# Decoding an output weight by columns and moving its decode phases into later steps (sparse attention followed by a token mix)

## The chip, the cores and the metric

The kernel runs on one core of one Trainium2 chip. The metric is the time of one launch in microseconds (us), measured on the device. Three runs of the kernel before gave 586.12 us in the median (585.53 to 589.59).

## The reference

Two parts follow each other. The first is block-sparse attention over 4 batches, 8 heads, 768 tokens and a head width of 64. The second is a mix over tokens on the result `x` (4 x 768 x 512):

```python
theta = x @ w_theta                       # 512 x 512
zr, zi = x * cos(theta), x * sin(theta)
y = einsum('ts,bsd->btd', w_tok_r, zr) + einsum('ts,bsd->btd', w_tok_i, zi)
u = x + y
return u + maximum(u @ w_ch, 0)           # w_ch is 512 x 512
```

The weights are float64 (q, k and v float32). The host only rearranges them, so the kernel itself turns the 64-bit words of each weight into pairs of fp32r tiles (a high part and a low part). A product with such a weight takes three matmuls: high by high, high by low, low by high.

## The kernel before, in words

**Decoding.** A `Piece` (line 50) is a run of columns of one weight: it loads the words (`load`, line 61, a DMA on SP's queue into a `raw` tile, two buffers), and is then decoded in three phases. Phase 0 is one ACT instruction (`start`, line 68) and three DVE instructions (`bits`, lines 72 to 74). Phase 1 is two DVE instructions (`rest`, lines 80 and 82). Phase 2 is one ACT copy that writes the high part (`high`, line 88) and two DVE instructions (`low`, lines 91 and 92), the second of which writes the low part. `Decoder.go(n)` (line 116) issues the next n phases; after the last phase of a piece it issues the load of the piece after next, since that one takes over its `raw` buffer. `Decoder.ahead(n)` (line 107) issues the ACT instructions that can go before.

**Which pieces.** Most weights are decoded during attention. Twelve pieces of 256 columns, 36 phases, are left for the token mix: four pieces hold the last 512 columns of `w_tok_r` and `w_tok_i` (columns 256 to 767 of the sixth token block, which only the product steps with j = 5 read), eight hold `w_ch`. Its tile is `[128, 4, 512]`: four blocks c of input channels by 512 output columns. Before, a piece of `w_ch` is 256 consecutive elements of that tile read as one row, that is half of one block c.

**Steps.** `token_mix` (line 586) runs 48 steps: k = 12 b + 6 h + j for batch b, half h of the channels and token block j. In step k, `theta(k + 2)` (12 matmuls of 256 columns), `reduced`, `waves`, `turned` (ACT and DVE work on the angles: range reduction, cosine and sine, product with x, split into high and low) prepare steps ahead; `turn` and `split` (DVE transposes, line 638, ACT cast, line 646, DVE difference, line 647) prepare x of step k + 3 where h is 0; `mix(k)` issues 24 matmuls of 384 columns that add into four accumulators `y` (lines 707 to 709). After j = 5, `add_x` (lines 720 to 723) makes `u`.

**Output products.** `out(b, th, e)` (line 725) makes 128 output columns e for 384 tokens th: 12 matmuls (lines 730 to 732) that read the column block e of all four blocks c of `w_ch`, then two DVE instructions (735 and 736) and a store on SP's queue. The eight products of a batch are put on `pending` at its last step and issued two by two in steps j = 1 to 4 of the next batch, in one PSUM buffer. The order is all four e for th = 0, then all four for th = 1.

**What sets the order.** Attention and the first five steps (`FIXED`, line 787) stand under a manual schedule: each engine gets them in the order of the program text. From step 5 on, a planner that simulates the engines orders the instructions of each engine, with the program text as priority; it also fills gaps of the manual part with work from later steps. Each engine's queue is then fixed and in order. `PHASES` (line 30) says how many phases each of the steps 0 to 12 gets: 2, 3, 3, 4, 4, 0, 4, 4, 4, 3, 3, 0, 2. The first 12 phases are the four `w_tok` pieces, so before they end with step 3.

In a fixed step the decode phases stand behind the step's other work and ahead of its products:

```python
turned(k + 1); split(k + 3); reduced(k + 2); load(k + 3); load_raw(k + 5)
decoder.ahead(PHASES[k]); decoder.go(PHASES[k])
mix(k)
```

Of the kernel before, what the change touches and what calls it, by code (L numbers as in the profile page):

```python
# [10 lines left out]
F32 = mybir.dt.float32  # L11
# [5 lines left out]
ALU = mybir.AluOpType  # L17
# [9 lines left out]
Q_BUFS = 3  # L27
XO_BUFS = 2
FIXED = 5
PHASES = (2, 3, 3, 4, 4, 0, 4, 4, 4, 3, 3, 0, 2)  # L30
LATER = 2560


# [16 lines left out]
class Piece:  # L50
# [4 lines left out]

    def __init__(self, nc, place, part, src, name):
        self.nc, self.place, self.part, self.src, self.name = nc, place, part, src, name
        self.f = src.shape[1] // 2
        self.before = None

    def load(self, pool, queue):
        self.raw = pool.tile([P, self.f, 2], I32, tag="raw", name=f"raw_{self.name}", bufs=2)
        queue.dma_start(self.raw, self.src.rearrange("p (f w) -> p f w", w=2))

    def start(self, pool):
        self.pool = pool
# [17 lines left out]
    def high(self):  # L84
        if self.before:
            self.before()
        self.hi, self.lo = [x.rearrange("p c f -> p (c f)")[:, self.part] for x in self.place]
        self.nc.scalar.copy(self.hi, self.a)

    def low(self):  # L90
        self.nc.vector.tensor_tensor(self.a, self.a, self.hi.bitcast(F32), op=ALU.subtract)
        self.nc.vector.tensor_tensor(self.lo, self.a, self.raw[:, :, 0].bitcast(F32), op=ALU.add)


class Decoder:
# [490 lines left out]
def token_mix(tc, w, ch_pieces, xs, outT, bias, nb, fore):  # L586
# [7 lines left out]
    nc = tc.nc  # L594
    with ExitStack() as late, ExitStack() as ctx:
# [4 lines left out]
        def at(k):  # L600
            return k // 12, (k // 6) % 2, k % 6

        def load(k):

            b, h, j = at(k)
            xa[k] = xp.tile([P, 4, 4, 32], F32, tag="xa", name=f"xa{k}")
            for i in range(4):
                src = xs[b // 2][4 * j + i, :, :, b % 2].rearrange("c q p f -> q c (p f)")
                dst = xa[k][32 * i : 32 * i + 32].rearrange("s (c p) x u -> s c (p x u)", c=2)
                nc.sync.dma_start(dst, src)  # L610

        def load_raw(k, pool=None, parts=range(4)):

            b, h, j = at(k)
            if h:
                return
            if pool is not None:
                xr[b, j] = pool[:, 512 * j : 512 * j + 512].rearrange("p (i c u) -> p i c u", i=4, c=4)
            else:
                xr[b, j] = zp.tile([P, 4, 4, 32], F32, tag="xr", name=f"xr{b}_{j}", bufs=2)  # L620
            for p in parts:
                src = xs[b // 2][4 * j : 4 * j + 4, p // 2, :, b % 2, p % 2].rearrange("i q c -> q i c")
                nc.sync.dma_start(xr[b, j][32 * p : 32 * p + 32].rearrange("r i c u -> r i (c u)"), src)
# [69 lines left out]
        def turned(k):  # L693
            multiplied(k)
            highs(k)
            lows(k)
# [28 lines left out]
        def out(b, th, e, pool, tag):  # L725
            ps = pool.tile([P, 384], F32, tag=tag, name=f"o{b}_{th}_{e}")
            wh, wl = [x[:, :, 128 * e : 128 * e + 128] for x in w["ch"]]
            for c in range(4):
                uh, ul = [t[:, c % 2, :] for t in us[b, c // 2, th]]
                nc.tensor.matmul(ps, wh[:, c, :], uh, start=c == 0, stop=False)  # L730
                nc.tensor.matmul(ps, wh[:, c, :], ul, start=False, stop=False)  # L731
                nc.tensor.matmul(ps, wl[:, c, :], uh, start=False, stop=c == 3)  # L732
            uh, ul = [t[:, e % 2, :].bitcast(F32) for t in us[b, e // 2, th]]
            o = wk.tile([P, 384], F32, tag="o", name=f"of{b}_{th}_{e}")
            nc.vector.tensor_tensor(o, uh, ul, op=ALU.add)
            nc.vector.scalar_tensor_tensor(o, ps, 0.0, o, op0=ALU.max, op1=ALU.add)
            nc.sync.dma_start(outT[b, 128 * e : 128 * e + 128, 384 * th : 384 * th + 384], o)

        vp = yield
        place = vp.tile([P, 6, 260], F32, tag="vw", name="xr_first").rearrange("p c f -> p (c f)")  # L740
# [5 lines left out]
        decoder = Decoder(ch_pieces(), None, nc.sync, fore)  # L746
# [5 lines left out]
        for k in range(2):  # L752
            load(k)
# [19 lines left out]
        split(2)  # L773
        highs(0)
        load(2)
        yield
        lows(0)
# [8 lines left out]
        pending = []  # L786
        for k in range(FIXED):
# [7 lines left out]
            load_raw(k + 5)  # L795
            phases = PHASES[k]
            decoder.ahead(phases)
# [6 lines left out]
        for k in range(FIXED, steps):  # L804
            b, h, j = at(k)
            if k + 4 < steps:
                load(k + 4)
            if k + 5 < steps:
                load_raw(k + 5)
            if k + 2 < steps:  # L810
                theta(k + 2)
                reduced(k + 2)
                waves(k + 2)
                turned(k + 2)
            if k + 3 < steps:
                turn(k + 3)
                split(k + 3)
            if k < len(PHASES):
                decoder.ahead(PHASES[k])
                decoder.go(PHASES[k])  # L820
            mix(k)
            if h == 0 and b > 0 and 0 < j < 5:
                for _ in range(2):
                    out(*pending.pop(0), ps_o, "o")
            if h == 1 and j == 5:
                pending += [(b, th, e) for th in range(2) for e in range(4)]
        while pending:
            out(*pending.pop(0), ps_y, "y")

# [1 line left out]
def sparse_attention_then_token_mix(ctx, tc, qT, qE, kT, vr, sampled, w_theta, w_tok_r, w_tok_i, w_ch, outT):  # L831
    nc = tc.nc
    n_batch = outT.shape[0]
    const = ctx.enter_context(tc.tile_pool(name="const", bufs=1))
    ident = const.tile([P, P], F32, name="ident")
    make_identity(nc, ident)
    bias = []
    for name, value in (("half_pi", math.pi / 2), ("up_int", ROUND), ("down_int", -ROUND), ("early", 0.0)):
        bias.append(const.tile([P, 1], F32, name=name))
        nc.vector.memset(bias[-1], value)  # L840
    dram = ctx.enter_context(tc.tile_pool(name="dram", bufs=1, space=bass.MemoryType.DRAM))
    xs = [dram.tile([NB, 2, 32, 2, 2, P], F32, name=f"xs{bp}") for bp in range(NP)]

    w = {}
    w["theta"] = [const.tile([P, 4, 512], F32R, name=f"w_theta_{x}") for x in ("hi", "lo")]
    for name in ("tok_r", "tok_i"):
        w[name] = [const.tile([P, 2, 768], F32R, name=f"w_{name}_{x}") for x in ("hi", "lo")]

    def room(name, use, dtype=F32):
        return const.tile([P, 8, 768], dtype, tag=f"room_{name}", name=f"{use}_{name}")  # L850

    def settle(name):
        t = room(name, "w", F32R)
        w[name] = [x[:, j] for x in w[name] for j in range(2)]
        w[name] = [w[name][2 * x : 2 * x + 2] + [t[:, 4 * x + j] for j in range(4)] for x in range(2)]
        return [t[:, 4 * x : 4 * x + 4] for x in range(2)]

    words = {n: a.bitcast(I32) for n, a in dict(theta=w_theta, tok_r=w_tok_r, tok_i=w_tok_i, ch=w_ch).items()}

    def pieces(name, f, place, at=0, span=None):  # L860
        made = []
        first, last = span or (0, place[0].shape[1] * place[0].shape[2])
        for f0 in range(first, last, f):
            f1 = min(f0 + f, last)
            made.append(Piece(nc, place, slice(f0, f1), words[name][:, 2 * (at + f0) : 2 * (at + f1)], f"{name}_{at + f0}"))
        return made


    fore = ctx.enter_context(tc.tile_pool(name="fore", bufs=2))
    rests = dict(tok_r=[], tok_i=[])  # L870

    def mix_pieces():
        made = [x for n, place in rests.items() for x in pieces(n, 256, place, 1536, (LATER, 3072))]
        return made + pieces("ch", 256, w["ch"], span=(0, 2048))

    follow = token_mix(tc, w, mix_pieces, xs, outT, bias, n_batch, fore)
    next(follow)
    early = pieces("theta", 512, w["theta"])
    early += [x for pair in zip(pieces("tok_r", 512, w["tok_r"]), pieces("tok_i", 512, w["tok_i"])) for x in pair]
    for name, place in rests.items():  # L880
        made = pieces(name, 512, place, 1536, (0, LATER))
        made[0].before = lambda name=name, place=place: place.extend(settle(name))
        early += made
    attention(tc, qT, qE, kT, vr, sampled.bitcast(I32), xs, ident, early, room, follow)
    for _ in follow:
        pass
# [48 lines left out]
```

## Time and profile before

| | |
|---|---|
| three timed runs, median | 586.12 us (585.53 to 589.59) |
| profiled execution: its own time | 591.45 us |
| profiled execution: span from first to last instruction | 589.7 us |
| busy share of the span: PE, DVE, ACT, POOL | 92%, 75%, 58%, 26% |
| mean granted TensorE clock | 0.988 |
| decode instructions of `w_ch` (`da_ch` tiles) | first at 281.0 us, last at 339.7 us |
| output product matmuls (lines 730 to 732) | first at 290.0 us, last at 585.3 us |
| loads of `w_ch` words | 8 of 256 KB, issued from 276.8 to 322.3 us |

Times in the profile are us from the start of the span. PE is TensorE's matmuls and PEld its weight loads, which overlap matmuls; DVE is VectorE, ACT ScalarE, SPq the queue of SyncE that issues DMAs. A row of the timeline gives start, duration, engine, source line, operation, what it writes from what it reads, shape, and in brackets the idle time of the engine before it with what ended it. A row of a table by stretches gives for each engine its busy time and, in brackets, how many instructions, then the granted clock (PEclk), the share of DMA time and GB/s. Matmul ends are modelled.

### The profile page before, as it was taken

The numbers are of one execution on the slowest core, as the hardware profiler recorded it, in microseconds if no ns is written. First come the engines' busy times: TensorE is split into PE (matmuls) and PEld (weight loads), VectorE is DVE, ScalarE is ACT, GpSimd is POOL, SyncE is SP. The second block draws the span as 40 slices with busy tenths as digits, with TensorE's granted clock in tenths as the row PEclk, the third lists the DMA queues.
The fourth block names the chain that finished last, engine by engine and source line by source line (L and its number), as shares of the span: only waits on it lengthen the run. The fifth ranks groups of instructions, "written<-read, shape, count | busy, mean of one in ns | idle before, by whom it ended". The sixth has DMA issues, their size and how long they took to land.

```text
span 589.7 us, 16811 instructions
## 1 busy us (share of the span) xinstructions
PE 541.2 (92%) x6636; PEld 477.0 (81%) x6636; DVE 440.0 (75%) x1011; ACT 344.1 (58%) x734; POOL 150.7 (26%) x262
## 2 busy tenths in 40 slices
PE   4898887998988978989999999999999999999997
PEld 1565654666666656878998999999999999999997
DVE  2687985887889878889989996648857549547554
ACT  2686775858797868755766544456534547434510
POOL 1467885741689874000000000000000000000000
PEclk9998998999999989999999999999999999999999
DMA  8979999886799997544323242111432111212002
GB/s 288 345 207 329 287 353 359 266 256 243 218 303 302 301 303 208 138 133 126 107 72 107 83 143 82 58 50 55 131 94 68 50 53 43 79 56 73 4 1 107
DMA packets 63551, 95.60 MB, mean 162 GB/s; under 512 B 9200, under 2 KB 44656, under 8 KB 63472
## 3 DMA queue, kind: packets, MB, share of 16 engines
q1 hardware_dynamic: 57136, 71.09, 39.1%
q0 software_dynamic: 6336, 23.43, 12.1%
q8 instruction: 52, 0.85, 0.6%
q14 instruction: 27, 0.22, 0.1%
HBM read 81.90 MB, written 12.58 MB: 160 GB/s over the span
## 4 chain that ended last, share of the span: by engine, by line
PE 59%; DVE 15%; issue 6%; POOL 6%; ACT 5%; DMA 3%; POOLq 2%; SPq 2%; DVEq 0%; ACTq 0%
PE y L709 8%; PE y L707 8%; PE y L708 8%; POOL kg L270 5%; PE o L731 4%; PE o L732 4%; PE o L730 4%; PE T L326 4%; PE X L360 3%; PE S L309 3%; PE h L657 3%; PE h L655 3%; PE h L656 3%; PE SW L402 2%; DVE m L311 2%
## 5 line engine op out<-in xcount | busy, mean ns | idle before, releaser
L320 ACT ACTIVATE P<-S,m 128x256 f32<-128x256 f32 x176 | 69.2, 486 | 6.6 <-DVE m L311 6.3
L328 ACT COPY pT<-T 128x1024 f32<-128x1024 f32 x44 | 44.7, 1017 | 33.2 <-PE T L326 32.6
L311 DVE TENSOR_REDUCE m<-S 128x4 f32<-128x1024 f32 x44 | 53.5, 1217 | 13.3 <-PE S L309 13.2
L326 PE MATMUL T<-ident,P 128*128 128x128 f32 x352 | 52.5, 291 | 9.3 <-ACT P L320 3.2
L270 POOL COPY kg<-kb 128x256 f32 (+2 forms) x101 | 53.3, 569 | 16.2 <-PE S L309 16.1
L270 POOL COPY kg<-kb_tok_i 128x256 f32 (+2 forms) x101 | 50.8, 543 | 25.2 <-DVE sb_scratch L176 15.2
L326 PEld LDWEIGHTS T<-ident,P 128*128 128x128 f32 x352 | 40.3, 147 | 21.0 <-ACT pT L328 10.9
L662 ACT ACTIVATE t<-h,up_int 128x256 f32<-128x256 f32 x48 | 22.6, 473 | 57.2 <-PE h L657 55.9
L655 PE MATMUL h<-w_theta_hi,xTh 128*128 128x256 f32 x192 | 54.3, 283 | 1.7 <-ACT xTh L646 1.7
L657 PE MATMUL h<-w_theta_hi,xTl 128*128 128x256 f32 x192 | 54.1, 282 | 0.4 <-DVE xTl L647 0.4
L309 PE MATMUL S<-kg,q 64*32 64x256 f32 x1408 | 51.0, 393 | 3.7 <-issue 2.2
L292 POOL DMA_INDIRECT vb<-in_vr_dram,rows x44 | 44.5, 1012 | 37.3 <-PE X L360 31.2
L656 PE MATMUL h<-w_theta_lo,xTh 128*128 128x256 f32 x192 | 53.9, 281 | 0.0
L707 PE MATMUL y<-w_tok_r,zh 128*128 128x384 f32 x128 | 43.3, 338 | 2.2 <-ACT zh L687 2.2
L731 PE MATMUL o<-ul,w_ch_hi 128*128 128x384 f32 x128 | 43.0, 336 | 0.4 <-DVE ul L723 0.4
L708 PE MATMUL y<-w_tok_i,zh 128*128 128x384 f32 x128 | 43.1, 337 | 0.0
L709 PE MATMUL y<-w_tok_r,zl 128*128 128x384 f32 x128 | 43.1, 337 | 0.0
L707 PE MATMUL y<-w_tok_i,zh 128*128 128x384 f32 x128 | 43.1, 336 | 0.0
L708 PE MATMUL y<-w_tok_r,zh 128*128 128x384 f32 x128 | 43.0, 336 | 0.0
L732 PE MATMUL o<-uh,w_ch_lo 128*128 128x384 f32 x128 | 42.9, 335 | 0.0
L672 ACT ACTIVATE cs<-rr 128x256 f32<-128x256 f32 x48 | 20.0, 416 | 39.3 <-DVE rr L667 39.3
L730 PE MATMUL o<-uh,w_ch_hi 128*128 128x384 f32 x128 | 42.5, 336 | 0.0
(155 smaller groups left out, 1432.1 us busy)
## 6 DMA issues: line engine op xcount, KB each, us to landing
xa<-xs SPq DMA_DIRECT2D x192, 64.0 KB
out_dram<-of SPq DMA_DIRECT2D x32, 192.0 KB
va<-in_vr_dram SPq DMA_DIRECT2D x22, 260.0 KB
q<-in_qT_dram SPq DMA_DIRECT2D x22, 256.0 KB
xs<-xo SPq DMA_DIRECT2D x88, 64.0 KB
xr<-xs SPq DMA_DIRECT2D x84, 64.0 KB
raw_tok_r<-in_w_tok_r_dram SPq DMA_DIRECT2D x8, 512.0 KB
raw_tok_i<-in_w_tok_i_dram SPq DMA_DIRECT2D x8, 512.0 KB
```

Of the source, the lines that this page charges most:

```text
L270: nc.gpsimd.tensor_copy(dst, blocks.rearrange("r g s f -> r s g f"))
L309: nc.tensor.matmul(sc[32 * p : 32 * p + 32, e, b, :], q[rows, b, p, :], keys[rows, :, :, place(b, p), :], start=True, stop=True)
L320: nc.scalar.activation(pt[:, e, b, :], sc[:, e, b, :], AF.Exp, bias=m[:, e, b : b + 1], scale=-1.0)
L326: nc.tensor.transpose(t[:, k, :], pt, ident)
L655: nc.tensor.matmul(ps, hi[:, c, :], wh[:, c, :], start=c == 0, stop=False)
L656: nc.tensor.matmul(ps, hi[:, c, :], wl[:, c, :], start=False, stop=False)
L657: nc.tensor.matmul(ps, lo[:, c, :], wh[:, c, :], start=False, stop=c == 3)
L707: nc.tensor.matmul(acc, zh[:, dd], wh[j][:, tt], start=j == 0 and m == 0, stop=False)
L708: nc.tensor.matmul(acc, zh[:, dd], wl[j][:, tt], start=False, stop=False)
L709: nc.tensor.matmul(acc, zl[:, dd], wh[j][:, tt], start=False, stop=j == 5 and m == 1)
L731: nc.tensor.matmul(ps, wh[:, c, :], ul, start=False, stop=False)
L732: nc.tensor.matmul(ps, wl[:, c, :], uh, start=False, stop=c == 3)
```

## The change

Four edits. `w_ch` is cut into eight other pieces: each holds the same 128 output columns of two blocks c, so two pieces make one column block e complete; they are decoded in order of e. A piece still has 256 elements per partition, but its place in the tile is two runs of 128, and its words lie in memory as two runs of 1 KB per partition instead of one of 2 KB (`shaped`, and the load's view). The four `w_tok` pieces keep their cut. `PHASES` becomes 1, 1, 2, 4, 4, 0, 1, 3, 3, 1, 1, 0, 0, 3, 3, 3, and in steps 14 and 15 three more phases stand between the two output products; so the `w_tok` pieces end with step 4, and of the 24 phases of `w_ch` 9 are issued by step 10 and 15 in steps 13 to 15. The output products of the first batch are issued by columns (e, then th); for the other batches the order stays.

```diff
-PHASES = (2, 3, 3, 4, 4, 0, 4, 4, 4, 3, 3, 0, 2)
+PHASES = (1, 1, 2, 4, 4, 0, 1, 3, 3, 1, 1, 0, 0, 3, 3, 3)
...
-        self.f = src.shape[1] // 2
+        self.c = src.shape[1]
+        self.f = self.c * src.shape[2]
...
-        queue.dma_start(self.raw, self.src.rearrange("p (f w) -> p f w", w=2))
+        queue.dma_start(self.raw.rearrange("p (c f) w -> p c f w", c=self.c), self.src)
...
-        self.hi, self.lo = [x.rearrange("p c f -> p (c f)")[:, self.part] for x in self.place]
-        self.nc.scalar.copy(self.hi, self.a)
+        self.hi, self.lo = [self.part(x) for x in self.place]
+        self.nc.scalar.copy(self.hi, self.shaped(self.a))
+
+    def shaped(self, x):
+        return x.rearrange("p (c f) -> p c f", c=self.c)
 
     def low(self):
-        self.nc.vector.tensor_tensor(self.a, self.a, self.hi.bitcast(F32), op=ALU.subtract)
-        self.nc.vector.tensor_tensor(self.lo, self.a, self.raw[:, :, 0].bitcast(F32), op=ALU.add)
+        a = self.shaped(self.a)
+        self.nc.vector.tensor_tensor(a, a, self.hi.bitcast(F32), op=ALU.subtract)
+        self.nc.vector.tensor_tensor(self.lo, a, self.shaped(self.raw[:, :, 0].bitcast(F32)), op=ALU.add)
...
             if h == 0 and b > 0 and 0 < j < 5:
-                for _ in range(2):
+                for x in range(2):
                     out(*pending.pop(0), ps_o, "o")
+                    if x == 0 and j > 1:
+                        decoder.ahead(3)
+                        decoder.go(3)
             if h == 1 and j == 5:
-                pending += [(b, th, e) for th in range(2) for e in range(4)]
+                pending += [(b, th, e) for e in range(4) for th in range(2)]
+                if b:
+                    pending.sort()
...
-            made.append(Piece(nc, place, slice(f0, f1), words[name][:, 2 * (at + f0) : 2 * (at + f1)], f"{name}_{at + f0}"))
+            part = lambda x, f0=f0, f1=f1: x.rearrange("p c f -> p (c f)")[:, f0:f1].unsqueeze(1)
+            src = words[name][:, 2 * (at + f0) : 2 * (at + f1)].rearrange("p (c f w) -> p c f w", c=1, w=2)
+            made.append(Piece(nc, place, part, src, f"{name}_{at + f0}"))
         return made
+
+    def channel_pieces():
+        whole = words["ch"].rearrange("p (c f w) -> p c f w", c=4, w=2)
+        parts = [(slice(c, c + 2), slice(128 * e, 128 * e + 128)) for e in range(4) for c in (0, 2)]
+        return [Piece(nc, w["ch"], lambda x, c=c, f=f: x[:, c, f], whole[:, c, f], f"ch_{c.start}_{f.start}") for c, f in parts]
...
-        return made + pieces("ch", 256, w["ch"], span=(0, 2048))
+        return made + channel_pieces()
```

## The prediction

> **What bounds the kernel now.** I read the page's head first, then the table by stretches, then the timeline of PE around its idle times, then DVE, ACT and SP's queue at the same places.
>
> ```profile
> span 589.7 us, 16811 instructions
> PE 541.2 (92%) x6636; PEld 477.0 (81%) x6636; DVE 440.0 (75%) x1011; ACT 344.1 (58%) x734; POOL 150.7 (26%) x262
> ```
>
> PE is the busiest engine, so the question is where it still waits. The table by stretches (columns: PE, PEld, DVE, ACT, POOL busy, granted clock, DMA share, GB/s):
>
> ```profile
> 210.00:220.00 10.00, 7.73 (x174) 5.83 (x175) 7.03 (x14) 5.35 (x12) 6.90 (x12) 0.84 1.00 295
> 245.60:340.00 94.40, 89.03 (x553) 86.22 (x554) 85.29 (x263) 56.89 (x144) 0.00 (x0) 1.00 0.38 107
> 340.00:580.00 240.00, 240.00 (x1494) 240.00 (x1493) 157.57 (x407) 109.76 (x257) 0.00 (x0) 1.00 0.22 67
> 330.00:340.00 10.00, 9.14 (x60) 8.95 (x59) 10.00 (x33) 6.82 (x16) 0.00 (x0) 1.00 0.33 97
> 340.00:350.00 10.00, 10.00 (x63) 10.00 (x62) 9.38 (x29) 5.10 (x13) 0.00 (x0) 1.00 0.51 148
> 350.00:360.00 10.00, 10.00 (x62) 10.00 (x62) 5.62 (x17) 3.63 (x10) 0.00 (x0) 1.00 0.39 119
> 360.00:370.00 10.00, 10.00 (x63) 10.00 (x62) 8.94 (x22) 4.56 (x11) 0.00 (x0) 1.00 0.22 68
> ```
>
> The token mix starts its products at 245.6 us. From 340 us on PE never pauses, and the change adds or removes no matmul: after that point time can only be lost. From 245.6 to 340 us DVE is busy 85.29 of 94.40 us, and PE idles 94.40 - 89.03 = 5.37 us by its matmuls and 94.40 - 86.22 = 8.18 us by its weight loads. All that the change can win lies between these two, about 1% of the launch; attention, where the clock once fell to 0.84, has the same instructions as before.
>
> The Trainium skill ("Perfetto Trace Analysis", section Identifying the Most-Contended Engine) calls matmul busy time a bad measure of headroom, since matmuls are pipelined, and takes weight-load busy time instead. By that rule the ceiling would be the 8.18 us alone, 586.12 - 8.18 = 577.9 us. I keep both ends, since the modelled tail of the last matmul hides part of each pause and a weight load can also be early.
>
> PE's single pauses, with what ended them:
>
> ```profile
> 256.53 0.39 PE L655 MATMUL h<-w_theta_hi,xTh 128*128 128x256 f32 x1 [0.94 <-ACT xTh L646]
> 257.25 0.39 PE L657 MATMUL h<-w_theta_hi,xTl 128*128 128x256 f32 x1 [0.22 <-DVE xTl L647]
> 263.66 0.39 PE L655 MATMUL h<-w_theta_hi,xTh 128*128 128x256 f32 x1 [0.78 <-ACT xTh L646]
> 264.38 0.39 PE L657 MATMUL h<-w_theta_hi,xTl 128*128 128x256 f32 x1 [0.22 <-DVE xTl L647]
> 279.73 0.45 PE L707 MATMUL y<-w_tok_r,zh 128*128 128x384 f32 x1 [1.38 <-ACT zh L687]
> 334.13 0.45 PE L707 MATMUL y<-w_tok_r,zh 128*128 128x384 f32 x1 [0.86 <-ACT zh L687]
> ```
>
> Three places in the fixed steps make up 1.16 + 1.00 + 1.38 = 3.54 us of the 5.37; the other 1.83 us are small ones, the last of them at 334 us. By weight loads everything is 8.18 / 5.37 = 1.52 times as long.
>
> **The change part by part.** No instruction disappears; decode phases go to later places of DVE's and ACT's queues. What stands in front of the first two pauses:
>
> ```profile
> 253.32 0.29 DVE L80 TENSOR_SCALAR ds_tok_r<-da_tok_r 128x256 int32<-128x256 int32 x1
> ...
> 253.99 0.89 DVE L638 STREAM_TRANSPOSE r<-xr 128x128 f32<-128x128 f32 x4
> ...
> 258.55 0.42 DVE L91 TENSOR_TENSOR da_tok_r<-da_tok_r,w_tok_r 128x256 f32<-128x256 f32 x1
> 259.00 0.42 DVE L92 TENSOR_TENSOR w_tok_r<-da_tok_r,raw_tok_r 128x256 fp32r<-128x256 f32 x1
> 259.34 0.29 DVE L72 TENSOR_SCALAR da_tok_r<-da_tok_r 128x256 f32<-128x256 f32 x1
> ...
> 260.45 0.30 DVE L80 TENSOR_SCALAR ds_tok_r<-da_tok_r 128x256 int32<-128x256 int32 x1
> ...
> 261.13 0.88 DVE L638 STREAM_TRANSPOSE r<-xr 128x128 f32<-128x128 f32 x4
> ```
>
> (1) Step 0 gives up one of two phases, `rest` (253.32 to 253.99, 0.67 us); it goes behind the transposes on which xTh waits. PE's pause at 256.53 shrinks by 0.67 us. What stays of it is the `bits` of the first phase and the cast.
>
> (2) Step 1 had three phases, 258.55 to 261.13 = 2.58 us, and keeps one (`rest`, 0.67). The transposes come 1.91 + 0.67 = 2.58 us earlier, PE only 0.67. The lead of 1.91 us is more than the pause at 263.66 and 264.38, 1.00 us (1.52 by weight loads): it goes wholly, and I take 1.25.
>
> (3) Step 2 has two phases instead of three (`low`, 0.79, and `bits`, 1.11, against 2.58: 0.68 saved), step 3 four in both. The four of step 3 before stood ahead of the `turned` that feeds the products of step 5:
>
> ```profile
> 275.45 0.42 DVE L91 TENSOR_TENSOR da_tok_i<-da_tok_i,w_tok_i 128x256 f32<-128x256 f32 x1
> ...
> 278.48 0.42 DVE L92 TENSOR_TENSOR w_tok_i<-da_tok_i,raw_tok_i 128x256 fp32r<-128x256 f32 x1
> 278.82 0.42 DVE L682 TENSOR_TENSOR cs<-cs,xa 128x256 f32<-128x256 f32 x1
> ...
> 281.64 0.42 DVE L666 SCALAR_TENSOR_TENSOR rr<-t,rr 128x256 f32<-128x256 f32 x1
> ```
>
> DVE reaches 278.82 about 0.67 + 1.91 + 0.68 = 3.3 us earlier, PE 1.9: the pause of 1.38 us (2.10) closes. But these same four phases, 275.45 to 278.82 = 3.4 us, are now in step 4, behind the angles of the next step. They finish `w_tok_i`, which the second half of step 5's products reads. From the first product of x (278.82) DVE needs 2.8 us to line 666 at 281.64, 0.7 us more, then 3.4: 6.9 us. PE starts 0.9 us after that (279.73) and has 24 products, 3.9 us at the mean of 240.00 / 1494 = 0.161 us; it may pull in angle products of later steps, so it waits 0 to 2 us for the last piece. I take 1.0. Net: 1.7 - 1.0 = 0.7 us won, from 2.1 won to 0.6 lost.
>
> (4) Steps 5 to 12 carry 9 phases of `w_ch` instead of 20, and before they were fed late:
>
> ```profile
> 303.93 0.36 SPq L63 DMA_DIRECT2D raw_ch<-in_w_ch_dram  x1
> 304.34 6.90 SPq L610 DMA_DIRECT2D xa<-xs  x5
> ...
> 307.46 0.43 ACT L68 ACTIVATE da_ch<-raw_ch 128x256 f32<-128x256 f32 x1 [2.14 <-DMA raw_ch<-in_w_ch_dram]
> ...
> 315.18 0.43 ACT L68 ACTIVATE da_ch<-raw_ch 128x256 f32<-128x256 f32 x1 [2.69 <-DMA raw_ch<-in_w_ch_dram]
> ...
> 307.93 0.29 DVE L72 TENSOR_SCALAR da_ch<-da_ch 128x256 f32<-128x256 f32 x1 [2.01 <-ACT da_ch L68]
> ```
>
> A load is issued only when the piece before last is done, takes 3.5 us (303.93 to 307.46), and meanwhile ACT stands at line 68 with the sines behind it, and DVE idles 2.01 us. With one piece every two or three steps the words are there in time. The small pauses, 1.83 us (2.8), lose their two causes, a full DVE and a held ACT; how much returns no row can say. I take two thirds of the middle, 1.5 us, and keep 0 and 2.8 as ends.
>
> (5) Steps 13 to 15 take in 15 phases, five pieces. Dependent instructions give 2.58 us a piece (above), five 12.9 us. Where independent ones alternate they start closer together than they last:
>
> ```profile
> 299.42 0.30 DVE L80 TENSOR_SCALAR ds_ch<-da_ch 128x256 int32<-128x256 int32 x1
> 299.62 0.57 DVE L723 TENSOR_TENSOR ul<-uf,uh 128x384 fp32r<-128x384 f32 x1
> ```
>
> 0.20 us for a 0.30 one, and 259.00 to 259.34, 0.34, for a 0.42 one: three of the first and four of the second kind make 1.96 us a piece, 9.8 in all. A step with two output products has 60 matmuls, 9.7 us of PE at 0.161. From 340 to 370 us DVE is busy 9.38 + 5.62 + 8.94 = 23.9 of 30 us, so 9.8 more make 33.7: up to 3.7 us over, part of which is backlog that the change itself removes. PE has a stock against it, since angles are prepared two steps ahead. The nearest row is 330 to 340, where DVE was full and PE lost 0.86; I take 0.9 lost, with ends 0 and 3.7. Each column is finished a step before its products, about 10 us, so I charge no wait of PE for it.
>
> (6) Views and transfers. A column piece is written as two runs of 128. Row by row the shapes that exist already say that this costs nothing (strided xTh and xTl against contiguous `w_theta`):
>
> ```profile
> L646 ACT CAST xTh<-r 128x512 fp32r<-128x512 f32 x24 | 14.7, 620 | 5.9 <-DVE r L638 4.5 <-DVE uf L720 1.3
> L88 ACT CAST w_theta_hi<-da_theta 128x512 fp32r<-128x512 f32 x4 | 2.5, 632 | 0.0
> ```
>
> The eight loads move 256 KB as before in twice as many runs. Their SP issue of 0.36 us may double; SP's queue is past it (it stood 6.90 us over five issues above, mostly waiting). If that cover is gone, a piece's words come 0.4 us later, against a spare step. On SP these loads now also stand among the stores of output products, which wait for DVE. Issuing the first batch's products by columns changes no count.
>
> **Sum.** -0.67 - 1.25 - 0.7 - 1.5 + 0.9 = -3.2 us. The profiled execution took 591.45 us (span 589.7), 5.3 above the median; the terms lie in stretches at full clock, so I carry them over: 591.45 becomes 588.2, and the median 586.12 becomes **582.9 us**. The ends: -0.67 - 1.52 - 2.1 - 2.8 = -7.1, 579.0 us; -0.67 - 1.0 + 0.6 + 0 + 3.7 = +2.6, 588.7 us.
>
> **The rivals.**
>
> R1, everything comes back. DVE ceases to bind at all; only the 1.16 - 0.67 = 0.5 us of the first pause stays. Between 4.9 and 7.7 us won, middle 6.3: 579.8 us. For it: the lead of DVE grows from step to step. Against: step 5 meets its last piece late, and one DVE still has 85 of 94 us to do at first.
>
> R2, the pauses only change their cause. The planner has already pulled transposes of the next batch into the fixed steps; this cast belongs to one and itself waited for DVE:
>
> ```profile
> 265.62 0.62 ACT L646 CAST xTh<-r 128x512 fp32r<-128x512 f32 x1 [0.46 <-DVE r L638]
> ```
>
> If it fills the freed DVE time with more of that, or issues the phases written in steps 14 and 15 earlier as fillers, so that the move does not do what it says, only (1) and (5) remain: -0.67 + 0.9, 586.4 us.
>
> R3, slower: ACT is held for raw words in steps 13 to 15. Five pieces follow each other through two buffers, behind stores on SP that wait for DVE; each late load holds ACT 2.14 to 2.69 us as at 307 and 315, and with it the next step's angles. It decides as soon as more than the 4.1 us won in (1) to (4) reach PE, that is two holds; with three, 3 x 2.69 = 8.1 us in place of 0.9: 586.1 - 4.1 + 8.1 = 590.1 us. For it: five such waits in the trace of before, 8.0 us in all.
>
> ```profile
> ACT da_ch L68 <- DMA raw_ch<-in_w_ch_dram: 8.0, 5, 2.7
> ```
>
> Against: there the loads were a piece apart, now mostly a step.
>
> **How the numbers follow.** A measurement of this kernel tells about 1%, 5.9 us, from no change. Forecast 0.48 (582.9, its own spread 580.5 to 585.5), R1 0.18, R2 0.22, R3 0.12. Faster by over 1% (below 580.3): most of R1 and a little of the forecast, 0.18. Slower by over 1% (above 592.0): half of R3, 0.06. Within 1%: 0.76. The range goes from the low end, 579.0, to the high end with the edge of R3, 588.9; it leaves out some of R1 and most of R3, under 2 in 10.
>
> **What would show it.** Right: the pauses before lines 655 and 657 in the second and third fixed step gone or under 0.7 us; the first product of step 5 without a pause, a shorter one within it that ends on line 92 or 88; `da_ch` work last seen some 20 us or more later than 339.7; PE idle between 245 us and the stretch that never pauses down from 5.4 to about 2 us; no idle of ACT at line 68 over 1 us. Wrong: new pauses of PE between 335 and 375 us that add up to more than 2 us (R3 if ACT line 68 stands behind them), or the same 5 us of idle with other releasers (R2).

## The result, and the profile after

The changed kernel took **582.99 us** in the median of 21 runs (579.12 to 589.85); beside it the kernel before took 588.2 us in 21 runs (582.9 to 593.54). The ratio is 0.992, interval 0.9894 to 0.9946. The forecast was a saving of 3.2 us, to 582.9 us. That the two times agree to 0.1 us is luck: the three runs that I started from have a median 2.1 us below that of the 21, and the change saved more than I had summed, 4.7 us by the ratio (3.2 to 6.2), 4.6 us in the traces below, where terms of the sum were wrong in both directions. A second timing, below, gave a ratio of 0.9985, 0.9 us, so the size of the saving rests on the traces. A ratio leaves out the executions that count as slow; the profiled execution of before (591.45 us) is one of these, the second profile of before below is not.

The profiled execution of the changed kernel took 584.26 us. The head of its page, for the same two lines of before:

```profile
span 582.5 us, 16818 instructions
PE 540.7 (93%) x6636; PEld 476.5 (82%) x6636; DVE 438.6 (75%) x1011; ACT 344.0 (59%) x734; POOL 152.6 (26%) x262
```

The same work is done (PE 540.7 us against 541.2). The table by stretches of the changed kernel (PE, PEld, DVE, ACT, POOL busy, granted clock, DMA share, GB/s):

```profile
210.00:220.00 10.00, 8.87 (x218) 6.18 (x204) 9.49 (x16) 8.41 (x17) 9.51 (x15) 1.00 0.92 279
245.60:340.00 94.40, 92.18 (x589) 91.09 (x588) 86.66 (x267) 59.94 (x150) 0.00 (x0) 1.00 0.38 112
330.00:340.00 10.00, 10.00 (x67) 10.00 (x66) 9.48 (x33) 6.90 (x17) 0.00 (x0) 1.00 0.46 133
340.00:350.00 10.00, 10.00 (x60) 10.00 (x59) 8.98 (x29) 4.26 (x12) 0.00 (x0) 1.00 0.39 120
350.00:360.00 10.00, 10.00 (x65) 10.00 (x64) 6.85 (x17) 3.37 (x9) 0.00 (x0) 1.00 0.33 93
360.00:370.00 10.00, 10.00 (x63) 10.00 (x63) 8.31 (x20) 5.45 (x13) 0.00 (x0) 1.00 0.26 80
```

From 245.6 to 340 us PE's idle time falls from 5.37 to 2.22 us by matmuls and from 8.18 to 3.31 us by weight loads. From 330 us on, where I had charged 0.9 us for a fuller DVE, PE loses nothing, and DVE is no fuller than before (8.98 + 6.85 + 8.31 = 24.1 us of 30, 23.9 before). What still pauses, on PE's timeline of the changed kernel (lines of its program; five more than before from the token mix on):

```profile
253.72 0.39 PE L662 MATMUL h<-w_theta_hi,xTl 128*128 128x256 f32 x1 [0.22 <-DVE xTl L652]
273.69 0.44 PE L712 MATMUL y<-w_tok_r,zh 128*128 128x384 f32 x1 [0.41 <-ACT zh L692]
280.34 0.41 PE L712 MATMUL y<-w_tok_r_hi,zh 128*128 128x384 f32 x1 [0.39 <-DVE uf L725]
284.24 0.44 PE L712 MATMUL y<-w_tok_r_hi,zh 128*128 128x384 f32 x1 [1.19 <-ACT zh L692]
```

The pauses of 0.78 and 0.86 us and of the 0.94 us at 256.53 are gone, the 1.38 before step 5 is 0.41, and two are new: 0.39 and 1.19 us, before the first products of steps 6 and 7.

**A measure that holds still.** The first product of step 0 (line 707, after 712) came at 245.61 us in the first profile of before and at 243.25 us here, though attention's instructions stand in the same order on every engine. In the fourteen profiles of this case (those of the experiments included) it came between 239.59 and 250.21 us; one visible part of that is the clock. Up to that product the mean granted clock was 0.97 in six of the profiles, which took 243.14 to 250.21 us, and 0.98 to 1.00 in the other eight, which took 239.59 to 244.15 us. (From 210 to 220 us it was 0.84 in the first profile of before and 1.00 here; both are among the six, so the clock does not explain the 2.36 us between them.) So I compare the kernels from that product on. I split this at the first products of steps 5, 12 and 24, found by the order of the instructions on PE. Here is the table by stretches of before, cut so:

```profile
245.61:279.73 34.12, 30.58 (x192) 29.32 (x193) 29.36 (x93) 17.68 (x44) 0.00 (x0) 1.00 0.48 133
279.73:319.57 39.84, 39.45 (x246) 38.83 (x247) 35.49 (x109) 26.21 (x71) 0.00 (x0) 1.00 0.33 93
319.57:404.95 85.38, 83.94 (x523) 83.00 (x524) 64.53 (x178) 44.66 (x106) 0.00 (x0) 1.00 0.27 81
```

And of the changed kernel:

```profile
243.25:273.69 30.44, 29.80 (x193) 29.33 (x193) 25.86 (x84) 16.96 (x41) 0.00 (x0) 1.00 0.49 136
273.69:314.72 41.03, 39.45 (x246) 38.83 (x247) 38.90 (x119) 29.46 (x77) 0.00 (x0) 1.00 0.34 101
314.72:397.76 83.04, 83.04 (x524) 83.04 (x523) 63.30 (x178) 42.46 (x102) 0.00 (x0) 1.00 0.27 81
```

The reader is to compare the first number of each row with its weight-load time: PEld is the same in both kernels (29.3, 38.8, 83.0 us), and what a row is longer than that is what PE lost. Before that was 4.80 + 1.01 + 2.38 = 8.19 us, after it is 1.11 + 2.20 + 0.00 = 3.31 us: 4.88 us won, and the stretches themselves are 4.83 us shorter (159.34 to 154.51). All profiles, cut in the same way (us; each number is the length of that stretch):

| kernel | steps 0 to 4 | 5 to 11 | 12 to 23 | 24 to the end | first product to end | ratio to before, timed |
|---|---|---|---|---|---|---|
| before | 34.12 | 39.84 | 85.38 | 184.75 | 344.09 | |
| before, second profile | 32.42 | 39.61 | 85.58 | 184.73 | 342.34 | 1.0022 [0.9985, 1.006] |
| before, third profile | 33.30 | 39.68 | 85.52 | 184.76 | 343.26 | |
| after | 30.44 | 41.03 | 83.04 | 184.74 | 339.25 | 0.992 [0.9894, 0.9946] |
| after, second profile | 29.37 | 40.95 | 83.04 | 184.68 | 338.04 | 0.9985 [0.9952, 1.0019] |
| after, third profile | 29.90 | 41.09 | 83.04 | 184.67 | 338.70 | |
| fixed phases alone | 30.00 | 40.67 | 83.59 | 184.69 | 338.95 | 0.9953 [0.9922, 0.9984] |
| all but the fixed phases | 32.47 | 38.97 | 83.55 | 184.72 | 339.71 | 0.9961 [0.9925, 0.9997] |
| columns alone | 32.50 | 39.42 | 83.69 | 184.68 | 340.29 | 1.0007 [0.9979, 1.0035] |
| columns alone, again | 32.50 | 39.21 | 83.93 | 184.70 | 340.34 | 0.9942 [0.9908, 0.9976] |
| one phase back in step 1 | 31.60 | 41.45 | 83.18 | 184.74 | 340.97 | 0.9945 [0.9912, 0.9978] |
| five late pieces bare | 30.83 | 41.19 | 83.21 | 184.74 | 339.97 | 0.993 [0.99, 0.9959] |
| all pieces bare | 28.05 | 42.80 | 82.97 | 184.72 | 338.54 | 0.9898 [0.9847, 0.9948] |
| late words by POOL | 29.38 | 40.68 | 83.67 | 184.35 | 338.08 | 0.9945 [0.9915, 0.9975] |

In the means of three profiles the change won 33.28 - 29.90 = 3.38 us in steps 0 to 4, gave back 41.02 - 39.71 = 1.31 us in steps 5 to 11, and won 85.49 - 83.04 = 2.45 us in steps 12 to 23, in all 343.23 - 338.66 = 4.57 us. The three profiles of before lie 1.75 us apart, those of the changed kernel 1.21 us; the other rows are one profile each. A pause that ends on the first product of a stretch counts in the stretch before it.

### The profile page after: what moved, and what is told of

Read it like the earlier page. It is cut to its first block, busy times and chain, and to the rows that moved or that the text cites. A ratio compares the mean times of both kernels' runs of the same rounds, so it can differ in the third digit from the quotient of the medians.

```text
span 582.5 us, 16818 instructions
## 1 busy us (share of the span) xinstructions
PE 540.7 (93%) x6636; PEld 476.5 (82%) x6636; DVE 438.6 (75%) x1011; ACT 344.0 (59%) x734; POOL 152.6 (26%) x262
## 4 chain that ended last, share of the span: by engine, by line
PE 68%; DVE 14%; ACT 7%; issue 4%; DMA 4%; SPq 3%; ACTq 0%; DVEq 0%
PE y L712 10%; PE y L714 10%; PE y L713 10%; PE T L331 5%; PE X L365 4%; PE o L736 4%; PE o L737 4%; PE o L735 4%; PE S L314 3%; PE h L662 3%; PE h L661 3%; PE h L660 3%; ACT P L325 3%; DVE m L316 3%; PE SW L407 2%
## 5 line engine op out<-in xcount | busy, mean ns | idle before, releaser
L275 POOL COPY kg<-kb_tok_i 128x256 f32 (+2 forms) x101 | 52.0, 554 | 24.6 <-DVE sb_scratch L182 15.0
L314 PE MATMUL S<-kg,q 64*32 64x256 f32 x1408 | 53.2, 397 | 2.2 <-issue 2.1
```

The lines of the kernel that those rows point to most:

```text
L275: nc.gpsimd.tensor_copy(dst, blocks.rearrange("r g s f -> r s g f"))
L314: nc.tensor.matmul(sc[32 * p : 32 * p + 32, e, b, :], q[rows, b, p, :], keys[rows, :, :, place(b, p), :], start=True, stop=True)
```

## The experiments

The theory to test was the forecast's: the gain is a sum of separate shares, one from the fixed steps, one from the decode that steps 5 to 12 lose, less a charge for the 15 late phases. The rivals: one part alone carries all of it, or what the two first profiles show is a difference of two executions.

**The two kernels once more.** Each was run against before again, unedited, with a profile, and then profiled a third time in a single execution.

> The kernel before itself, as a control, and for a second profile. The stretch up to the first product of step 0 has the same order of instructions in all kernels, yet took 239.6 to 250.2 us in nine profiles. If that is chance (half-clock windows of 3.4 us), the ratio is 1.000 within its interval, and what tells the kernels apart is the stretch from the first product to the end: 344.1 us in the first profile of before, 339.3 in that of the changed kernel. Theory A: this stretch repeats within 1 us. Rival: the first profile of before had an unlucky pause in step 1 (0.94 us before line 655, absent in the two experiments with the same first two steps), and the stretch is 340 to 342 us here.

> The changed kernel again, for a second profile and a time beside the control. Ratio 0.992 as on record, 0.989 to 0.995; from the first product to the end 338.5 to 340 us; no pause of PE over 0.3 us in the fixed steps, and one of 0.8 to 1.6 us between steps 5 and 8.

> Third profile of the kernel before: first product to end 343 to 345 us by theory A, 340 to 342 us by the rival; pauses of 1.2 to 1.6 us before step 5 either way.

> Third profile of the changed kernel: first product to end 338.5 to 340 us either way.

Timed: before against itself 588.05 us, ratio 1.0022 [0.9985, 1.006]; after 585.33 us, ratio 0.9985 [0.9952, 1.0019]. The single executions took 588.18 and 581.13 us. The intervals of the changed kernel's two ratios do not even overlap, so the interval of one timing does not cover what differs from one timing to the next (not every timing was made on the same chip, and nothing here tells the chip from chance); the stretches do agree, within 1.8 us for before and 1.2 for after. PE's pauses in the second profile of before:

```profile
242.86 0.41 PE L707 MATMUL y<-w_tok_r_hi,zh 128*128 128x384 f32 x1 [0.34 <-DVE xo L345]
259.21 0.38 PE L655 MATMUL h<-w_theta_hi,xTh 128*128 128x256 f32 x1 [0.78 <-ACT xTh L646]
259.94 0.38 PE L657 MATMUL h<-w_theta_hi,xTl 128*128 128x256 f32 x1 [0.23 <-DVE xTl L647]
275.28 0.44 PE L707 MATMUL y<-w_tok_r,zh 128*128 128x384 f32 x1 [1.37 <-ACT zh L687]
```

No pause stands where the first profile had 0.94 us at 256.53 (10.9 us after its first product, here that would be 253.8); in the third 0.12 us of it is left, and 0.23 before line 657. The 0.78 and the 1.37 us come in every profile of before. So the pause of term (1), at the size that I had counted, belonged to that one execution; why it varies is open.

**The fixed phases alone**, in the kernel before, with pieces by rows:

```diff
-PHASES = (2, 3, 3, 4, 4, 0, 4, 4, 4, 3, 3, 0, 2)
+PHASES = (1, 1, 2, 4, 4, 0, 4, 4, 4, 3, 3, 4, 2)
```

> The kernel before with another PHASES alone: 1, 1, 2, 4, 4 in the fixed steps as in the changed kernel, and all 24 phases of w_ch, still cut by rows, in steps 6 to 12 (4, 4, 4, 3, 3, 4, 2). Theory A (two separate savings: about 3.7 us from the pauses of the fixed steps, of which about 1.2 is given back while the last w_tok piece is late, and about 2.5 us from the late decode): 2 to 3 us faster than before, ratio 0.995 to 0.9965, and PE's pauses before lines 655 and 657 gone. Theory B (DVE bounds steps 0 to 12 as a whole, so a pause removed early comes back later): within 0.5 us of before, ratio 0.999 to 1.001, with as much PE idle between the first product and step 14 as before, 5 us.

Timed 585.25 us, ratio 0.9953 [0.9922, 0.9984]. Its stretches:

```profile
244.15:274.15 30.00, 29.61 (x192) 29.41 (x192) 25.90 (x84) 17.00 (x41) 0.00 (x0) 1.00 0.51 136
274.15:314.82 40.67, 39.08 (x244) 38.40 (x245) 38.90 (x118) 29.54 (x77) 0.00 (x0) 1.00 0.34 99
314.82:398.41 83.59, 83.59 (x527) 83.59 (x526) 63.95 (x178) 42.64 (x103) 0.00 (x0) 1.00 0.29 83
```

Steps 0 to 4 and 5 to 11 are those of the changed kernel (29.90 and 41.02), with the same new pauses of 0.39 and 1.19 us: gain and give-back there belong to the fixed phases. But steps 12 to 23 are 1.9 us shorter too, with rows and without one phase written after step 12. PE loses nothing in them: they are 0.55 us longer than the changed kernel's because three matmuls more fall into them (527 against 524), and three fewer into the two stretches ahead. From the first product to the end this one line reaches 338.95 us, 343.23 - 338.95 = 4.28 of the 4.57 us.

**All but the fixed phases**, in the changed kernel:

```diff
-PHASES = (1, 1, 2, 4, 4, 0, 1, 3, 3, 1, 1, 0, 0, 3, 3, 3)
+PHASES = (2, 3, 3, 4, 4, 0, 1, 1, 1, 1, 1, 0, 0, 3, 3, 3)
```

> The changed kernel with the old phases in the fixed steps: PHASES = 2, 3, 3, 4, 4, 0, 1, 1, 1, 1, 1, 0, 0, 3, 3, 3 (columns and the 15 late phases kept). Theory A: the three pauses of the fixed steps are back and only the late decode saves, 2 to 3 us faster than before, ratio 0.995 to 0.9965. Theory B: what counts is how much DVE work stands before step 13, here as little as in the changed kernel, so all of the gain, 4.7 us, ratio 0.992.

Timed 586.69 us, ratio 0.9961 [0.9925, 0.9997]. Steps 0 to 4 are those of before without the accident (32.47 us; pauses of 0.79, 0.22 and 1.38 us), steps 5 to 11 have no pause between matmuls at all (38.97), steps 12 to 23 take 83.55 us.

**The columns alone**, all phases where they were:

```diff
-PHASES = (1, 1, 2, 4, 4, 0, 1, 3, 3, 1, 1, 0, 0, 3, 3, 3)
+PHASES = (2, 3, 3, 4, 4, 0, 4, 4, 4, 3, 3, 0, 2)
```

> The changed kernel with the old PHASES (2, 3, 3, 4, 4, 0, 4, 4, 4, 3, 3, 0, 2): column pieces, 1 KB runs and the first batch's products by columns, but nothing moved late. Theory A: the cut itself costs and gains nothing, ratio 0.998 to 1.002. Rival: the products of the first batch can be finished earlier as column 0 is complete after two pieces, and that alone fills PE's pauses at 319 to 334 us: 1.5 to 2.5 us faster, ratio 0.996 to 0.9975.

Timed 588.0 us, ratio 1.0007 [0.9979, 1.0035], against a stretch of 340.29 us that says 2.9 us won. The two disagree, so it was run again, unedited:

> The columns and the views alone, with every phase where it was before, timed once more in more rounds, because its first ratio (1.0007) and its stretch from the first product of step 0 to the end (340.29 us, against 342.34 to 344.09 in three profiles of the kernel before) disagree. If the stretch tells the truth (the order of the pieces alone takes away the small pauses of the output steps), the ratio is about 0.996 and the stretch 340 to 341 us again. If the first ratio does (the columns alone are worth nothing), the ratio is 0.999 to 1.002 and the stretch is 342 us or more.

Timed 585.12 us, ratio 0.9942 [0.9908, 0.9976]; the stretch is 340.34 us. Its stretches in the second profile:

```profile
241.46:273.96 32.50, 30.11 (x193) 29.39 (x193) 29.38 (x93) 17.70 (x44) 0.00 (x0) 1.00 0.47 131
273.96:313.17 39.21, 39.21 (x247) 38.86 (x247) 36.38 (x112) 26.78 (x72) 0.00 (x0) 1.00 0.34 98
313.17:397.10 83.93, 83.86 (x525) 83.19 (x523) 63.48 (x175) 43.72 (x104) 0.00 (x0) 1.00 0.28 81
```

The stretch repeated and the ratio did not, so I go by the stretch; the first timing came out high. So the fixed phases alone and the columns alone, which share no line, each take 1.6 to 1.9 of the 2.45 us out of steps 12 to 23, and so do all edits but the fixed phases. By weight loads PE idles there 2.38 to 2.58 us in the three profiles of before, nothing with the fixed phases alone, 0.34 us with all edits but these and 0.35 and 0.74 us with the columns alone. These savings do not add up: what before lost there hung on its own order of the instructions, and each of the three edits breaks it. Of the rivals, that one part carries all is nearly true of the fixed phases (4.28 of 4.57 us, from one profile), but not in the sense that the rest is worth nothing: alone it wins 3.5 us.

**One phase back in step 1**, taken from step 4:

```diff
-PHASES = (1, 1, 2, 4, 4, 0, 1, 3, 3, 1, 1, 0, 0, 3, 3, 3)
+PHASES = (1, 2, 2, 4, 3, 0, 1, 3, 3, 1, 1, 0, 0, 3, 3, 3)
```

> The changed kernel with one phase moved from step 4 to step 1: PHASES = 1, 2, 2, 4, 3, then as changed. Theory A: step 1 has 1.9 us of slack and hides 1.1 us more, the last w_tok piece ends 0.7 us earlier and step 5's products are less torn apart: 0.3 to 0.8 us faster than the changed kernel, ratio to before 0.9905 to 0.9915. Theory B: no difference from the changed kernel, 0.992.

Timed 584.71 us, ratio 0.9945 [0.9912, 0.9978], and a miss as an improvement: the stretch is 340.97 us, 2.3 more than after. PE's pauses:

```profile
273.93 0.44 PE L712 MATMUL y<-w_tok_r,zh 128*128 128x384 f32 x1 [1.58 <-ACT zh L692]
280.93 0.44 PE L735 MATMUL o<-uh,w_ch_hi 128*128 128x384 f32 x1 [0.74 <-ACT uh L727]
285.00 0.39 PE L660 MATMUL h<-w_theta_hi,xTh 128*128 128x256 f32 x1 [0.62 <-DVE rr L670]
```

The pause before step 5 is back (1.58 us, 1.38 before), and the give-back stays: which fixed step holds a phase matters there.

**Five late pieces bare.** In the changed kernel the last five pieces of `w_ch` lose their DVE instructions (35), and their low part becomes an ACT copy, so that these columns are not decoded:

```diff
...
+        if self.bare:
+            return self.nc.scalar.copy(self.lo, a)
...
+        late = channel_pieces()
+        for x in late[3:]:
+            x.bare = True
...
```

> The changed kernel without the DVE work of the five late pieces (bits, rest and low left out: 35 DVE instructions, 9.8 to 12.9 us; the low part is a copy by ACT instead, so w_ch is not decoded there). It measures what the 15 late phases cost in steps 13 to 15. Theory A (they lie wholly beside PE's products, which have a stock of two steps): the same time as the changed kernel within 0.5 us, ratio to before 0.991 to 0.9925. Rival (the predicted 0.9 us, up to 3.7, is really paid): 0.9 to 3.7 us faster than the changed kernel, ratio 0.986 to 0.9905.

Timed 583.37 us, ratio 0.993 [0.99, 0.9959]; stretch 339.97 us. Without the work of the 15 late phases on DVE the kernel is no shorter than with it (338.66 in the mean), and in steps 12 to 23 PE loses nothing with it or without it. Where I charged 0.9 us, they are free.

**All pieces bare.** In the kernel before, all twelve pieces lose their 84 DVE instructions, so nothing of the last `w_tok` columns and of `w_ch` is decoded:

```diff
...
+        if self.bare:
+            return self.nc.scalar.copy(self.lo, self.a)
...
+        for x in made:
+            x.bare = True
...
```

> The kernel before without the DVE work of all twelve pieces in the token mix (84 DVE instructions left out, the low part is a copy by ACT, so the last columns of w_tok and all of w_ch are not decoded). It is the most that any placing of the phases could win. Theory A (most of PE's 5.4 to 8.2 us of idle is due to these phases): 6 to 8 us faster than before, ratio 0.9865 to 0.990. Rival (other DVE work of steps 0 to 12 keeps PE waiting anyway): no faster than the changed kernel, ratio 0.991 to 0.993.

Timed 582.92 us (6 runs), ratio 0.9898 [0.9847, 0.9948]; stretch 338.54 us, that of the changed kernel. This is not a floor, though. PE has one pause after its first product, of 2.35 us, and the timeline shows where it comes from (ACT, DVE, PE in this order):

```profile
276.89 0.43 ACT L69 ACTIVATE da_ch<-raw_ch 128x256 f32<-128x256 f32 x1 [2.60 <-DMA raw_ch<-in_w_ch_dram]
...
277.76 0.43 DVE L688 TENSOR_TENSOR cs<-cs,xa 128x256 f32<-128x256 f32 x1 [2.54 <-ACT cs L679]
...
280.35 0.44 PE L713 MATMUL y<-w_tok_r_hi,zh 128*128 128x384 f32 x1 [2.35 <-ACT zh L693]
```

ACT stands 2.60 us at a piece's first instruction, because its words are not there; the cosine behind it is late, DVE waits 2.54 us for it, PE 2.35. That is R3's mechanism, ahead of step 6 of another kernel: this one hold of 2.60 us cost PE 2.35 us. Without it the weight-load times leave 338.54 - (70.85 - 68.29) = 336.0 us, so the changed kernel has not reached the floor:

```profile
242.66:270.71 28.05, 28.05 (x180) 28.05 (x181) 20.62 (x62) 19.88 (x50) 0.00 (x0) 1.00 0.56 154
270.71:313.51 42.80, 40.45 (x261) 40.24 (x259) 29.50 (x78) 30.45 (x84) 0.00 (x0) 1.00 0.35 100
```

These are the two first stretches of this kernel (70.85 us together, weight loads 68.29; the first is shorter also because 12 loads moved from it to the second).

**The late words by POOL.** In the changed kernel, the loads of all eight `w_ch` pieces go to POOL's queue, past the stores (the expectation below speaks of six; the trace shows eight on POOL):

```diff
-                self.pieces[k // 3 + 2].load(self.raws, self.queue)
+                piece = self.pieces[k // 3 + 2]
+                piece.load(self.raws, piece.nc.gpsimd if piece.name[:2] == "ch" else self.queue)
```

> The changed kernel with the last six loads of w_ch words issued by POOL, which has nothing to do in the token mix, instead of standing in SP's queue behind loads and stores. It tests the holds of ACT at its line 69 for raw words, 7.5 us in 7 times in the changed kernel. Theory A (PE has a stock, the holds reach nothing): holds shorter, time the same within 0.5 us, ratio to before 0.991 to 0.993. Rival (the holds are part of what is left): 0.6 to 2 us faster than the changed kernel, ratio 0.9885 to 0.991.

Timed 584.09 us, ratio 0.9945 [0.9915, 0.9975]; stretch 338.08 us, inside the changed kernel's 338.04 to 339.25. In the table of waits ACT's holds did not go away, they grew from 7.5 us in 7 to

```profile
ACT da_ch L69 <- DMA raw_ch<-in_w_ch_dram: 11.6, 6, 3.3
```

Taking the loads off SP's queue did not bring the words earlier; with two buffers a load can only be issued when the piece before last is done. The traces show this: in the changed kernel each of the last six loads is issued 0.06 to 0.38 us after the last decode instruction of the piece before last ends, and here 0.54 us after it. Of the 11.6 us of holds one reached PE. The cast of x stands behind it on ACT, at 319.95 us:

```profile
319.61 0.44 ACT L69 ACTIVATE da_ch<-raw_ch 128x256 f32<-128x256 f32 x1 [1.21 <-DMA raw_ch<-in_w_ch_dram]
...
320.61 0.39 PE L661 MATMUL h<-w_theta_hi,xTh 128*128 128x256 f32 x1 [0.36 <-ACT xTh L652]
```

By weight loads this pause is 0.68 us, all that PE lost in steps 12 to 23 here. The other holds cost PE nothing there. That the angles are far enough ahead is my reading; a third buffer, which would tell, was not tried.

## Why the prediction was right, and where it was wrong

The terms can be set beside the pauses that they were about. Here are their lengths by weight loads, in the three profiles of each kernel; the last column is what the means differ by:

| term | forecast, us | before | after | won, us |
|---|---|---|---|---|
| (1) pause at 256.53 and 257.25 | 0.67 won | 1.69, 0, 0.87 | 0.50, 0, 0 | 0.69 |
| (2) pause at 263.66 and 264.38 | 1.25 won | 1.53, 1.52, 1.53 | 0, 0, 0 | 1.53 |
| (3) pause before step 5 | 1.7 won | 1.58, 1.57, 1.57 | 0.61, 0, 0.57 | 1.18 |
| (3) wait for the late `w_tok_i` | 1.0 lost | 0, 0, 0 | 2.20, 2.23, 2.23 | -2.22 |
| (4) the small pauses of steps 5 to 23 | 1.5 won | 3.39, 3.29, 3.43 | 0, 0, 0 | 3.37 |
| (5) late phases in steps 13 to 15 | 0.9 lost | 0, 0, 0 | 0, 0, 0 | 0 |

The last column adds up to 4.55 us, the forecast to 3.22. Term (3) was 1.7 us too good and (4) and (5) together 2.8 us too bad, so the sum came out nearer than its terms.

**(1) and (2).** The mechanism was right: less decode in front of the transposes, and the pauses go. With the 1.7 us of (3) they made 0.67 + 1.25 + 1.7 = 3.62 us for steps 0 to 4; the first two profiles differ by 34.12 - 30.44 = 3.68, the means by 3.38. But term (1) was sized from an unlucky execution, so its size is luck: where its pause is missing, in the second profiles, 32.42 - 29.37 = 3.05 us are left, against 1.25 + 1.7 = 2.95.

**(3), wrong in size and in place.** I gave back 1.0 us for the late `w_tok_i`, with 2 us as the end. Steps 5 to 11 became 1.31 us longer, but they also lost a small pause of before (0.62 us, ahead of step 12); the two new pauses alone cost 0.68 + 1.52 = 2.20 us by weight loads:

```profile
280.31 0.19 PEld L712 LDWEIGHTS y<-w_tok_r_hi,zh 128*128 128x128 f32 x1 [0.68 <-ACT zh L692]
284.24 0.19 PEld L712 LDWEIGHTS y<-w_tok_r_hi,zh 128*128 128x128 f32 x1 [1.52 <-ACT zh L692]
```

They come with the same releasers in the kernel with the fixed phases alone, and in no kernel that keeps the old fixed phases and decodes all its words. And I expected a pause inside step 5 that ends on line 92 or 88. The planner instead split step 5's products (they run from 273.69 to 286.99 us) and let PE go on to steps 6 and 7. The decode of `w_tok_i` ended 11.7 us after step 5's first product, where I had summed 6.0, and stood, between instructions of `add_x`, in DVE's queue ahead of step 7's angles:

```profile
282.11 0.42 DVE L83 SCALAR_TENSOR_TENSOR raw_tok_i<-raw_tok_i,ds_tok_i 128x256 f32<-128x256 uint32 x1
282.45 0.42 DVE L96 TENSOR_TENSOR da_tok_i<-da_tok_i,w_tok_i 128x256 f32<-128x256 f32 x1
282.79 0.55 DVE L726 TENSOR_TENSOR uf<-uf,xTl 128x384 f32<-128x384 f32 x1
283.25 0.42 DVE L687 TENSOR_TENSOR cs<-cs,xa 128x256 f32<-128x256 f32 x1
```

DVE has no gap from 279.63 to 287 us; the product with x at 283.25 feeds the cast on which PE waits 1.19 us at 284.24. So the stall moved from the consumer of the decoded words to whoever stood behind them.

**(4) and (5), the mis-sized terms.** I forecast -1.5 + 0.9 = -0.6 us; steps 12 to 23 gave -2.45. Two things failed.

The first is the size of the pauses. The four last ones of before are 0.39 + 0.18 + 0.40 + 0.86 = 1.83 us between matmuls; I scaled them to 2.8 us by weight loads, and then took two thirds of the middle. Before, the weight loads themselves pause 0.62 + 0.51 + 0.72 + 1.05 = 2.90 us there:

```profile
319.54 0.19 PEld L707 LDWEIGHTS y<-w_tok_r_hi,zh 128*128 128x128 f32 x1 [0.62 <-ACT cs L673]
320.35 0.19 PEld L709 LDWEIGHTS y<-w_tok_r_hi,zl 128*128 128x128 f32 x1 [0.51 <-DVE zl L691]
323.90 0.19 PEld L731 LDWEIGHTS o<-ul,w_ch_hi 128*128 128x128 f32 x1 [0.72 <-DVE ul L723]
334.13 0.19 PEld L707 LDWEIGHTS y<-w_tok_r,zh 128*128 128x128 f32 x1 [1.05 <-ACT zh L687]
```

All four went, and at that length. Three of them lie in steps 12 to 23, which idle 85.38 - 83.00 = 2.38 us by weight loads, against 85.38 - 83.94 = 1.44 by matmuls; the stretch became 2.34 us shorter. The Trainium skill ("Perfetto Trace Analysis", section Identifying the Most-Contended Engine) judges PE's headroom by weight-load busy time, beside the share of peak arithmetic, and not by matmul busy time. Here the trace agrees, with 4.88 us of weight-load idle gone and 4.83 us won, while matmul idle over the same three stretches fell only from 5.37 to 2.22, by 3.15.

The second is the charge. The phases do not run where the text puts them. Here are steps 5 to 11 and steps 12 to 16 with the `da_ch` instructions alone (columns: DVE and ACT busy), of before:

```profile
279.73:319.57 39.84, 12.29 (x36) 5.32 (x13) 1.00 0.33 93
319.57:359.49 39.92, 4.31 (x13) 1.24 (x3) 1.00 0.39 113
```

and of the changed kernel:

```profile
273.69:314.72 41.03, 10.32 (x31) 4.59 (x11) 1.00 0.34 101
314.72:352.13 37.41, 5.79 (x18) 1.97 (x5) 1.00 0.36 109
```

The text moves 15 of 24 phases past step 12; of 48 DVE instructions only five moved past its first product (12 start behind it before, 17 after; one that straddles it counts in both rows), 1.5 us. Before, the text has all phases by step 12, and the planner had let the decode slip to 339.7 us; after, it drew part of it forward as a filler: five of the eight pieces are done by 314.56 us, where the text has three. That is the doing of R2 ("the move does not do what it says"), without its price. It also answers my sign "some 20 us or more later than 339.7", which failed:

```profile
L97 DVE TENSOR_TENSOR w_ch_lo<-da_ch,raw_ch x8: 414/419/421, 293.2 to 341.8; 128x256 fp32r<-128x256 f32 x8
```

Why before lost its 2.38 us is only argued. Just ahead of them, from 299.34 to 319.57 us, ACT was held for words (2.14 and 2.69 us, in the prediction's rows) and DVE idled, and between matmuls each pause ends on DVE or on an ACT cast behind it. DVE idles 4.1 to 4.4 us in steps 5 to 11 in the three profiles of before, and 1.8 to 3.3 us in every other kernel that decodes all its words. That fits, but every edit gives the planner another order, so no run took this hold away alone.

**(6), right.** The issue of a load on SP, before and then after (minimum, median and maximum in ns):

```profile
L63 SPq DMA_DIRECT2D raw_ch<-in_w_ch_dram x8: 351/362/745, 276.8 to 322.3; - x8
```

```profile
L64 SPq DMA_DIRECT2D raw_ch<-in_w_ch_dram x8: 389/390/396, 277.5 to 328.0; - x8
```

It rose by 28 ns in the median and did not double. Writing two runs of 128 costs nothing either: the ACT copy takes 392 ns in the median (400 before) and the last DVE instruction, in the row of L97 above, 419 (425 before). The columns alone cost PE no time.

**"No idle of ACT over 1 us", wrong.** It is still held, as before, without harm:

```profile
ACT da_ch L69 <- DMA raw_ch<-in_w_ch_dram: 7.5, 7, 2.7
```

Fewer pieces per step did not bring the words in time, since a load is issued when the piece before last is done, as seen above. So **R3** had its holds but not its price, which the bare kernel paid ahead of step 6. **R1** stays above what was reached: 3.31 us of weight-load idle are left in the first profile, 2.20 of them in the two new pauses.

## What to carry to other kernels

Cost a pause of PE by the weight loads of its stretch, not by the gaps between modelled matmuls, and compare two kernels from the first instruction of the stage that was changed. When a forecast hits, set each term beside its own pause: here two errors of opposite sign met. Under a planner, ask where an instruction runs, not where the text puts it: count it by stage in the trace before charging a move. A stall that is pushed later does not wait with the consumer you had in mind, it goes to whatever stands behind the late work in its engine's queue.

## What the runs showed of the hardware that was not expected

One and the same order of attention took between 239.59 and 250.21 us to the first product of the mix, more than twice what the whole change is worth, while the stretch after it repeated to 1.8 us, and its last part, from step 24 on, to 0.1 us in all but one profile (184.67 to 184.76; 184.35 with the loads on POOL). And one kernel, timed twice against before, gave 1.0007 [0.9979, 1.0035] and 0.9942 [0.9908, 0.9976].
